# Attention with routed experts on one core: the opening re-ordered and loaded over two queues, and two moves in VectorE's list

## The chip, the cores and the metric

The kernel runs on one core of one Trainium2 chip. TensorE (PE) multiplies matrices, VectorE (DVE), ScalarE (ACT) and GpSimd (POOL) work elementwise, and SyncE (SP) issues most of the transfers; ScalarE and GpSimd issue some as well. The metric is the device time of one execution in microseconds (us). A kernel is run several times and the median counts.

## The reference

```
scores = q @ k.T / sqrt(64)                      # 8 batches x 8 heads, 576 x 576, head size 64
cum    = cumsum(max(s, 0))                       # one gate row s of 576 values per head
scores = where(causal, -1e9, scores + min(-(cum_i - cum_j), 0))
attn   = softmax(scores);  x = attn @ v          # 4608 tokens of 512 values
logits = x @ w_gate;  e = argmax(logits)         # 8 experts, the best one only
out    = p_e * (max(x @ w1[e], 0) @ w2[e])       # 512 -> 1024 -> 512 per token
```

All data are float32. Products keep their accuracy by splitting a number into a rounded high part and a low part: low = number - high, so one product costs three matmuls.

## The kernel before

The 64 heads are taken as 32 pairs, two heads on the two halves of the 128 partitions. A pair goes through five groups of query rows (128 rows each and a mixed group of the last 64 of both heads). For a group g the program does S (scores: the gate term from `cu` and `pick`, then three matmuls from q and k, lines 238 onward), Z (VectorE adds the mask, negates and takes the row maximum, L278), X (ScalarE's exponential, L292), T (transposition on TensorE, L296), C (copy out of PSUM, L321 on VectorE and L322 on ScalarE) and, after all groups, AV (product with v, L332) and XB (copy of the result, L321). Scores live in a PSUM tile `s` of which there are two; a new S, or one of the routing steps RA to RD, may start when the older tile has been read.

Four pairs make a batch of tokens. Its routing runs in eight steps strewn into later rounds: gate products (L375), their transposition (L296, s<-ident,LT), `part`, `both`, `L`, `mx`, `dd` on VectorE (L389 to L406), an exponential on ScalarE (L408), one-hot rows, rank products (L427 to L430), the update of `base` (L436, L439) and `dsi` (L444), and scatters of rows into a table `xs` by GpSimd (L465). `scale` (L351 to L354) takes the reciprocals of the softmax sums; in VectorE's list it is called SC, and SE is the same work done once early, for the seventh of the eight batches.

Four strings in `ORDER`, one per engine, say in which order an engine takes its steps in a round, and how many rounds a step lags behind the first one (`Z1+2` is Z of group 1 of the pair two rounds back). `loop` walks them: an engine's next step is emitted as soon as what it needs has been emitted, so the lists alone set each engine's order.

The opening, `Attention.__init__`, prepares the gate terms: the rows s are loaded twice into `raw` (each half of the partitions holds one head, each copied), VectorE takes max (L138), a running sum (L139), the centres `cen` (L141, L144) and `low` (L147), ScalarE writes five centred copies `cu` (L177, `center`) and VectorE finishes each (L184, `build`). `split` rounds q and k of the first pair on ScalarE (L212, L218) and takes the low parts on VectorE (L215, L222; for later pairs on GpSimd). `raw`, `cum`, `zz` and `low` are parts of the tile `aT[1]`, so the order rows call them aT. Meanwhile TensorE runs products of zeros (L159) so that it is not idle before the first scores, and GpSimd writes masks and constants, among them those of `constants`, whose first part runs before the first round and whose other parts are taken by the step CO.

After the attention the experts run one after the other, TensorE nearly without a pause.

Of the kernel before, what the change touches and what calls it, by code (L numbers as in the profile page):

```python
# [8 lines left out]
F32 = mybir.dt.float32  # L9
# [4 lines left out]
AF = mybir.ActivationFunctionType  # L14
ALU = mybir.AluOpType
# [26 lines left out]
}  # L42
ZB = 4
RUNP = NPAIR
WARM = 24
FIRST = (0, 2, 1, 3, 5, 4)
EVAC = {0: "V", 1: "V", 2: "A", 3: "A", 4: "V"}
STEPS = (3, 0, 1, 4, 5, 6, 2, 7)
# [19 lines left out]
def after(tc, inst, names):  # L68
    ins = getattr(inst, "ins", inst)
    for name in names:  # L70
        tc.add_manual_dep(
            ins, name, mybir.DependencyInfo(mybir.DependencyClass.Sync, mybir.DependencyReason.DATA),
            reason="rows written before",
        )


class Attention:
    def __init__(self, ctx, tc, K, qkv, s, rt, ps_t):
        self.tc, self.nc, self.K, self.qkv, self.rt, self.ps_t = tc, tc.nc, K, qkv, rt, ps_t
# [24 lines left out]
        keep(nc.vector.tensor_reduce(
            out=self.sel, in_=K["ident"].rearrange("p (a c) -> p c a", c=32), op=ALU.add, axis=AX.X
        ))
        s4 = s.rearrange("(p h) c -> h p c", h=2)
        for x in range(4):
            nc.sync.dma_start(raw[32 * x : 32 * x + 32], s4[x // 2])
        self.load(0)  # L110
        for i in range(2):
            nc.scalar.activation(
                self.qd[i].rearrange("p a h c -> p (a h c)"), zz[:, : 4 * HP], AF.Copy
            )
        for x in range(4):
            nc.gpsimd.memset(sign[32 * x : 32 * x + 32, 0:1], 8.0 - 16.0 * (x % 2))
            nc.gpsimd.memset(sign[32 * x : 32 * x + 32, 1:2], 8.0 * (x % 2))
        nc.gpsimd.memset(self.half, 0.0)
        for h in range(2):
            nc.gpsimd.memset(self.half[64 * h : 64 * h + 64, h], 1.0)  # L120
        self.mask = cp.tile([P, 640], F32, name="mask")
        self.mask8 = cp.tile([P, S], F32, name="mask8")
        nc.gpsimd.memset(self.mask, 0.0)
        nc.gpsimd.memset(self.mask8, 0.0)
        nc.gpsimd.affine_select(
            out=self.mask[:, 512:], in_=self.mask[:, 512:], pattern=[[-1, P]],
            compare_op=ALU.is_ge, fill=BIG, base=0, channel_multiplier=1,
        )
        for h in range(2):
            r = slice(64 * h, 64 * h + 64)  # L130
            nc.gpsimd.affine_select(
                out=self.mask8[r, 512:], in_=self.mask8[r, 512:], pattern=[[-1, 64]],
                compare_op=ALU.is_ge, fill=BIG, base=0, channel_multiplier=1,
            )
        self.split(0, 5)
        for part in (0, 2):
            self.split(0, part)
        keep(nc.vector.tensor_scalar(out=raw, in0=raw, scalar1=0.0, scalar2=None, op0=ALU.max))  # L138
        keep(nc.vector.tensor_tensor_scan(out=cum, data0=raw, data1=zz, initial=0.0, op0=ALU.add, op1=ALU.add))  # L139
        mid = cum[:, TC[0] : TC[0] + 4 * TC[1] + 1 : TC[1]]  # L140
        keep(nc.vector.tensor_scalar(  # L141
            out=self.cen[:, 0], in0=mid, scalar1=sign[:, 0:1], scalar2=-1.0, op0=ALU.mult, op1=ALU.mult
        ))
        keep(nc.vector.tensor_scalar(out=self.cen[:, 1], in0=mid, scalar1=sign[:, 1:2], scalar2=None, op0=ALU.mult))  # L144
        for g in ORD:
            self.center(g)
        keep(nc.vector.tensor_scalar(out=low, in0=cum, scalar1=sign[:, 1:2], scalar2=None, op0=ALU.mult))  # L147
        for part in (1, 3):
            keep(self.split(0, part))
        self.build(ORD[0])  # L150
        self.build(ORD[1])
        self.build(ORD[2])
        self.split(0, 4)

        warm = self.ps_s.tile([P, 2, 512], F32, name="s")[:, 0]
        zb = zz.bitcast(BF16)
        for x in range(WARM):
            for c in ((0, 256), (256, 512)) if x % 3 == 0 else ((0, 512),):
                nc.tensor.matmul(  # L159
                    warm[:, c[0] : c[1]], zb[:, :P], zb[:, P + c[0] : P + c[1]],  # L160
                    start=True, stop=True, skip_group_check=True,
                )
        nc.gpsimd.memset(self.Es[MIX][:, S:], 0.0)
        self.LT = rt.tile([P, 640], F32, name="LT", bufs=1)
        nc.gpsimd.memset(self.LT[:, S:], 0.0)
        self.xb, self.sums, self.sumx, self.rr, self.ra = [], [], [], [], []
        for i in range(2):
            self.xb.append(rt.tile([P, 4, 640], F32, name=f"xb{i}", bufs=1))
            nc.gpsimd.memset(self.xb[i][:, :, S:], 0.0)
            self.sums.append(rt.tile([P, 4, 8], F32, name=f"sums{i}", bufs=1))  # L170
            self.sumx.append(rt.tile([P, 4], F32, name=f"sumx{i}", bufs=1))
            self.rr.append(rt.tile([P, 5, 8], F32, name=f"rr{i}", bufs=1))
            nc.gpsimd.memset(self.rr[i][:, 4], 1.0)
            self.ra.append(rt.tile([P, 2, 5, 4], F32, name=f"ra{i}", bufs=1))

    def center(self, g):
        self.nc.scalar.activation(  # L177
            self.cu[:, TO[g] : TO[g] + TW[g]], self.cum[:, : TW[g]], AF.Identity,
            scale=self.sign[:, 0:1], bias=self.cen[:, 0, g : g + 1],
        )  # L180

    def build(self, g):
        o = slice(TO[g], TO[g] + TW[g])
# [22 lines left out]
    def split(self, p, part):  # L206
        nc = self.nc
        d = self.st[p]
        q, k = d["x"][:, :S], d["x"][:, S:]
        if part == 0:  # L210
            d["q"] = self.lq.tile([P, 2, S], F32R, name="q")
            nc.scalar.activation(d["q"][:, 0], q, AF.Copy)  # L212
        elif part == 1:
            e = nc.gpsimd if p else nc.vector
            return e.tensor_tensor(out=d["q"][:, 1], in0=q, in1=d["q"][:, 0].bitcast(F32), op=ALU.subtract)  # L215
        elif part == 2:
            d["kh"] = self.ld.tile([P, S], F32R, name="kh")
# [400 lines left out]
    def loop(self):  # L618
# [3 lines left out]
        self.XR, self.rq, self.sq, self.chain = {}, [], [], None  # L622
        self.R = {b: dict(b=b, xb=self.xb[b % 2]) for b in range(RUNP // 4)}
        self.plan()
        self.todo = constants(self.nc, self.const, self.K, self.wg)
        self.unbuilt = list(ORD[3:])
        done = self.done = {(f"K{x}", 0) for x in range(6)} | {("LX", 0), ("LV", 0), ("LX", 1), ("LV", 1)}
        lists = [[(x.split("+")[0], int(x.split("+")[1])) for x in o.split()] for o in ORDER.values()]
# [359 lines left out]
            if more:  # L988
                self.tails(e, x4)

def constants(nc, cp, K, wg):
    blank = cp.tile([P, WIDE], F32, name="blank")[:, :ROW]
    nc.gpsimd.memset(blank[:, : DM + 1], 0.0)
    nc.gpsimd.iota(blank[:, DM + 1 :].bitcast(I32), pattern=[[0, 1]], base=1 << 20, channel_multiplier=0)
    K["blank"] = blank
    K["wg"] = cp.tile([P, 4, 32], F32, name="wg")
    nc.sync.dma_start(K["wg"], wg.rearrange("(k p) e -> p k e", p=P))

# [113 lines left out]
```

## Time and profile before

| What | us |
|---|---|
| three runs: median (lowest, highest) | 785.6 (785.55, 787.28) |
| the profiled execution, its own time | 784.42 |
| its span from the first to the last instruction | 782.7 |
| TensorE busy | 758.6 |
| VectorE, ScalarE, GpSimd busy | 477.2, 414.7, 219.6 |
| the granted TensorE clock over the span | 0.996 of full |

The profiled execution takes 1.7 us more than its span. A row of the timeline gives the start of an instruction, its duration, engine, line, operation, what it writes and reads, and in brackets how long the engine stood idle before it and what ended that wait. [...] The two ends of the attention matter here: the first 20 us, and the round that begins about 280 us in.

### The profile page before, as it was taken

Reading aid. Unit: us, or ns where it says so; the run is one execution under the profiler, and the core shown is the slowest. Engines: PE = TensorE matmul, PEld = TensorE weight load, DVE = VectorE, ACT = ScalarE, POOL = GpSimd, SP = SyncE. Lnnn points to the kernel's source line nnn. Section 1 sums busy time; section 2 is a strip of 40 time slices with the busy share of each in tenths; the row PEclk is TensorE's granted clock in tenths of the full one; section 3 lists DMA queues with packets and bytes.
Section 4 is the critical chain, followed back from the end, with each engine's and each line's share of the span. In section 5 each row is a group of like instructions: output and inputs, shape, how many; then the busy total and the mean of one; then the engine's idle time right before and its main releaser. Section 6 shows DMA issues by size and latency. Waiting matters only on the chain.

```text
span 782.7 us, 17835 instructions
## 1 busy us (share of the span) xinstructions
PE 758.6 (97%) x6972; PEld 624.4 (80%) x6972; DVE 477.2 (61%) x1247; ACT 414.7 (53%) x1002; POOL 219.6 (28%) x328
## 2 busy tenths in 40 slices
PE   7999999999999988999999999999999999999995
PEld 5888888888888867678788887888888888888874
DVE  7778989899999999655263544522642453633520
ACT  7998888888888866523251432412521431513410
POOL 7544455656564645321001011010011001010011
PEclk9999999999999999999999999999999999999998
DMA  7763234434343414575172642710630271720101
GB/s 263 220 217 99 96 123 131 137 116 150 103 151 107 163 53 149 189 242 201 49 249 95 212 153 87 273 44 16 218 134 28 97 259 57 255 95 22 54 29 41
DMA packets 43903, 105.24 MB, mean 134 GB/s; under 512 B 3983, under 2 KB 3983, under 8 KB 43792
## 3 DMA queue, kind: packets, MB, share of 16 engines
q1 hardware_dynamic: 35408, 80.13, 30.6%
q0 software_dynamic: 5936, 18.92, 6.5%
q10 hardware_dynamic: 2448, 4.74, 1.8%
q8 instruction: 67, 1.10, 0.6%
q14 instruction: 44, 0.36, 0.2%
HBM read 75.91 MB, written 28.12 MB: 133 GB/s over the span
## 4 chain that ended last, share of the span: by engine, by line
issue 37%; DMA 12%; PE 4%; another core or an unknown queue 4%; POOL 3%; DVE 2%; POOLq 1%; ACT 1%; DVEq 0%
DMA xs<-xr,dsi 6%; DMA out_dram<-y,xr 6%; POOL out_dram L853 2%; PE t L332 1%; PE ph L820 1%; PE s L238 1%; PE t L296 0%; DVE z L278 0%; ACT aT L322 0%; POOLq L946 0%; DVE dd L406 0%; POOLq L853 0%; DVE xb L321 0%; POOLq L1107 0%
## 5 line engine op out<-in xcount | busy, mean ns | idle before, releaser
L846 PE MATMUL py<-w2t,hT 128*128 128x512 f32 x768 | 181.3, 392 | 1.2 <-DVEq L960 1.2
L820 PE MATMUL ph<-xT,w1t 128*128 128x512 f32 x768 | 178.3, 391 | 0.6 <-PEq L949 0.6
L820 PEld LDWEIGHTS ph<-xT,w1t 128*128 128x128 f32 x768 | 143.2, 188 | 31.9 <-issue 2.3
L292 ACT ACTIVATE E<-z,m 128x128 f32<-128x128 f32 (+4 forms) x288 | 165.8, 580 | 3.1 <-DVE m L278 3.1
L846 PEld LDWEIGHTS py<-w2t,hT 128*128 128x128 f32 x768 | 142.6, 188 | 30.4 <-issue 1.5
L853 POOL DMA_INDIRECT out_dram<-y,xr x39 | 37.9, 972 | 393.6 <-DVE y L852 331.0
L278 DVE CUSTOM_DVE_ANT_0 z<-s,mask 128x128 f32<-128x128 f32 (+4 forms) x288 | 139.0, 516 | 6.4 <-ACT E L292 0.6
L852 DVE TENSOR_SCALAR y<-py,xr 128x512 f32<-128x512 f32 x35 | 26.3, 751 | 117.5 <-PE py L846 117.5
L332 PE MATMUL t<-aT,v 128*64 128x64 f32 (+2 forms) x1408 | 95.2, 291 | 0.1
L822 ACT ACTIVATE hT<-ph 128x512 fp32r<-128x512 f32 x64 | 38.1, 596 | 96.4 <-PE ph L820 96.0
L332 PEld LDWEIGHTS t<-aT,v 128*64 128x64 f32 x1408 | 66.6, 137 | 18.8 <-issue 2.8
L825 DVE SCALAR_TENSOR_TENSOR hT<-ph,hT 128x512 fp32r<-128x512 f32 x64 | 44.2, 690 | 60.7 <-ACT hT L822 60.6
L238 PE MATMUL s<-kh,q 64*128 64x512 f32 (+3 forms) x512 | 80.2, 318 | 0.0
L322 ACT COPY aT<-t 128x1024 f32<-128x1024 f32 x64 | 57.5, 898 | 38.0 <-PE t L296 38.0
L238 PE MATMUL s<-cu,pick 64*128 64x128 f32 (+4 forms) x320 | 71.9, 374 | 2.5 <-DVE base L439 1.2
L296 PEld LDWEIGHTS t<-ident,E 64*128 64x128 f32 x1600 | 63.8, 138 | 9.2 <-ACT E L292 2.7
L296 PE MATMUL t<-ident,E 64*128 64x64 f32 x1600 | 67.4, 223 | 2.4 <-ACT E L292 0.9
L730 ACT ACTIVATE xT<-t 128x512 fp32r<-128x512 f32 x32 | 18.4, 597 | 90.9 <-PE t L793 90.9
L321 DVE COPY aT<-t 128x256 f32<-128x256 f32 (+2 forms) x96 | 61.6, 641 | 3.9 <-PE t L296 3.5
L292 ACT ACTIVATION_READ_ACCUMULATOR E<-z,m 128x1 f32 x288 | 55.3, 192 | 0.0
L238 PEld LDWEIGHTS s<-cu,pick 64*128 64x128 f32 (+1 forms) x320 | 36.6, 186 | 22.3 <-issue 10.1
L215 POOL TENSOR_TENSOR q<-qk,q 128x576 fp32r<-128x576 f32 x31 | 44.2, 1426 | 32.1 <-ACT q L212 32.0
(159 smaller groups left out, 1016.6 us busy)
## 6 DMA issues: line engine op xcount, KB each, us to landing
raw<-in_w_dram SPq DMA_DIRECT2D x32, 1024.0 KB, 5.8
qk<-in_qkv_dram SPq DMA_DIRECT2D x32, 576.0 KB, 3.9
v<-in_qkv_dram SPq DMA_DIRECT2D x32, 320.0 KB, 4.3
xr<-xs SPq DMA_DIRECT2D x8, 1028.0 KB, 5.7
xs<-blank ACTq DMA_DIRECT2D x9, 514.0 KB, 5.8
xs<-blank SPq DMA_DIRECT2D x8, 514.0 KB, 4.3
xr<-xs SPq DMA_DIRECT2D x8, 514.0 KB, 8.6
xs<-xr,dsi POOLq DMA_INDIRECT x40, 3.4
```

Of the source, the lines that this page charges most:

```text
L215: return e.tensor_tensor(out=d["q"][:, 1], in0=q, in1=d["q"][:, 0].bitcast(F32), op=ALU.subtract)
L238: self.nc.tensor.matmul(out, terms[n][0], terms[n][1], start=n == 0, stop=n == len(terms) - 1, skip_group_check=True)
L278: ins = nc.vector.tensor_tensor_reduce(out=cut(z[:, :w]), in0=x, in1=mask, scale=-0.125, scalar=3.0e38, op0=ALU.add, op1=ALU.min, accum_out=m,
L292: nc.scalar.activation(out, z[:, :w], AF.Exp, bias=m, scale=-1.0, accum_out=total)
L296: self.nc.tensor.transpose(out, src[r], self.K["ident"][r, r])
L321: return self.nc.vector.tensor_copy(o, i)
L322: return self.nc.scalar.copy(o, i)
L332: nc.tensor.matmul(ps[64 * h : 64 * h + 64, bank, lo - 512 * bank : hi - 512 * bank], v[:, kt, h], self.aT[p % 2][:, kt, h, lo:hi], start= ...
L820: nc.tensor.matmul(ps, w[:, a, d, c], x[:, b, d], start=n == 0, stop=n == 11)
L825: nc.vector.scalar_tensor_tensor(out=h[:, 1, f], in0=ps, scalar=0.0, in1=h[:, 0, f].bitcast(F32), op0=ALU.max, op1=ALU.subtract)
L846: self.nc.tensor.matmul(ps, hT[:, a, f, c], w[:, b, f % 4], start=f == 0 and i == 0, stop=f == 7 and i == 2)
L853: disjoint(self.tc, "out", self.nc.gpsimd.indirect_dma_start(out=self.out, out_offset=IndirectOffsetOnAxis(ap=row[:, DM + 1 : DM + 2].bitc ...
```

## The change

In the opening the s rows are loaded by two transfers instead of four, one issued by SyncE and one by ScalarE, each with a source of two copies of 32 rows. q and k of the first pair become two transfers, again one on each queue. ScalarE takes the first centred copy before q and k, and VectorE finishes it before the low parts of q and k. GpSimd writes `half` first, then the first `pick`, and one mask, a strip of `E4` and the first constant wait for the low part of k (`begun`); strips of `LT`, `xb` and `rr` and the other constants move into later CO steps (`blanks`). The products of zeros are 18 blocks of 512 columns instead of 24, 14 of them cut into halves. In VectorE's list SE moves from the end of one round behind the RAd and RDd of the next, and CI moves ahead of Z2 and RCd.

```
-    "DVE": "RAd+4 RDd+4 C4+3 Z1+2 ... RBd+3 Z2+2 RCd+3 CI+3 C1+2 XB+3 Z0+1 CO+1 SE+3",
+    "DVE": "RAd+4 RDd+4 SE+4 C4+3 Z1+2 ... RBd+3 CI+3 Z2+2 RCd+3 C1+2 XB+3 Z0+1 CO+1",
-WARM = 24
+WARM = 18
...
+        nc.gpsimd.memset(self.half, 0.0)
+        for h in range(2):
+            nc.gpsimd.memset(self.half[64 * h : 64 * h + 64, h], 1.0)
         s4 = s.rearrange("(p h) c -> h p c", h=2)
-        for x in range(4):
-            nc.sync.dma_start(raw[32 * x : 32 * x + 32], s4[x // 2])
-        self.load(0)
+        x = self.ldx.tile([P, 2 * S], F32, name="qk")
+        for i, queue in enumerate((nc.sync, nc.scalar)):
+            queue.dma_start(raw[64 * i : 64 * i + 64], s4[i].unsqueeze(0).broadcast_to([2, 32, S]))
+        for i, queue in enumerate((nc.sync, nc.scalar)):
+            queue.dma_start(x[:, S * i : S * i + S], self.qkv[0][:, S * i : S * i + S])
+        self.st[0] = dict(x=x)
+        self.split(0, 5)
...
-        for g in ORD:
+        self.center(ORD[0])
+        for part in (0, 2):
+            keep(self.split(0, part))
+        for g in ORD[1:]:
             self.center(g)
         keep(nc.vector.tensor_scalar(out=low, in0=cum, scalar1=sign[:, 1:2], scalar2=None, op0=ALU.mult))
+        self.build(ORD[0])
         for part in (1, 3):
-            keep(self.split(0, part))
-        self.build(ORD[0])
+            ins = self.split(0, part)
+            keep(ins)
+        self.begun = getattr(ins, "ins", ins).name
+        after(tc, nc.gpsimd.memset(self.mask8, 0.0), [self.begun])
...
-            for c in ((0, 256), (256, 512)) if x % 3 == 0 else ((0, 512),):
+            for c in ((0, 256), (256, 512)) if x < 14 else ((0, 512),):
...
-        nc.gpsimd.memset(self.Es[MIX][:, S:], 0.0)
+        after(tc, nc.gpsimd.memset(self.Es[MIX][:, S:], 0.0), [self.begun])
...
+    def blanks(self):
+        nc = self.nc
+        rest = constants(self.tc, self.const, self.K, self.wg, self.begun)
+        yield next(rest)
+        nc.gpsimd.memset(self.LT[:, S:], 0.0)
+        for i in range(2):
+            nc.gpsimd.memset(self.xb[i][:, :, S:], 0.0)
+            nc.gpsimd.memset(self.rr[i][:, 4], 1.0)
+        yield
+        yield from rest
...
-        self.todo = constants(self.nc, self.const, self.K, self.wg)
+        self.todo = self.blanks()
...
-    nc.gpsimd.memset(blank[:, : DM + 1], 0.0)
+    after(tc, nc.gpsimd.memset(blank[:, : DM + 1], 0.0), [begun])
     nc.gpsimd.iota(blank[:, DM + 1 :].bitcast(I32), pattern=[[0, 1]], base=1 << 20, channel_multiplier=0)
     K["blank"] = blank
+    yield
```

ScalarE's instructions from the program's start, before (qd is a tile of zeros, cu the centred gate terms, kh and q the rounded k and q):

```order
L112 ACT_TABLE_LOAD
L112 ACTIVATE qd_107<-aT_115 128x256
L112 ACTIVATE qd_108<-aT_115 128x256
L212 ACTIVATE q<-qk 128x576
L218 ACTIVATE kh<-qk 128x576
L177 ACTIVATE cu<-aT_115,cen,sign 128x128
L177 ACTIVATE cu<-aT_115,cen,sign 128x256
```

The same engine and place now:

```order
L113 DMA aT_115<-in_s_dram 64x1x576
L115 DMA qk<-in_qkv_dram 128x576
L119 ACT_TABLE_LOAD
L119 ACTIVATE qd_107<-aT_115 128x256
L119 ACTIVATE qd_108<-aT_115 128x256
L191 ACTIVATE cu<-aT_115,cen,sign 128x128
L226 ACTIVATE q<-qk 128x576
L232 ACTIVATE kh<-qk 128x576
L191 ACTIVATE cu<-aT_115,cen,sign 128x256
```

Two transfers stand at the head, and the first cu stands ahead of q and kh.

VectorE in the round that begins about 280 us in, before (rr and ra are the reciprocals of the sums, t and base belong to the ranks):

```order
L278 ISA z,m<-s,mask 128x128
L278 ISA m 128x1
L351 TENSOR_SCALAR rr_221<-sums_219 128x32
L351 TENSOR_SCALAR rr_221<-sumx_220 64x4 x2
L352 RECIPROCAL rr_221<-rr_221 128x32
L353 RECIPROCAL rr_221<-rr_221 64x8
L354 COPY ra_223<-rr_221 128x40
L436 TENSOR_TENSOR t_6275<-s,base 128x40
L439 TENSOR_TENSOR base<-base,s 128x8
L321 COPY aT_114<-t 128x2x5x64
```

The same place now:

```order
L292 ISA z,m<-s,mask 128x128
L292 ISA m 128x1
L450 TENSOR_TENSOR t_6268<-s,base 128x40
L453 TENSOR_TENSOR base<-base,s 128x8
L365 TENSOR_SCALAR rr_218<-sums_216 128x32
L365 TENSOR_SCALAR rr_218<-sumx_217 64x4 x2
L366 RECIPROCAL rr_218<-rr_218 128x32
L367 RECIPROCAL rr_218<-rr_218 64x8
L368 COPY ra_219<-rr_218 128x40
L335 COPY aT_114<-t 128x2x5x64
```

The update of base stands ahead of the gate sums, which were ahead of it.

VectorE later in the same round, before (part, both, L, mx and dd are the routing's logits, z the scores of group 2, xr a batch's scaled rows):

```order
L389 TENSOR_TENSOR part<-s,ra_223 128x160 x2
L278 ISA z,m<-s,mask 128x384
L278 ISA m 128x1
L278 ISA z,m<-s,mask 128x384
L278 ISA m 128x1
L454 TENSOR_TENSOR xr<-s,rr_221 128x2x4x64
L397 TENSOR_TENSOR both<-part 128x160
L399 TENSOR_REDUCE L<-both 128x40
L405 TENSOR_REDUCE mx<-L 128x5
L406 TENSOR_TENSOR dd<-L,mx 128x40
L321 COPY aT_115<-t 128x2x4x64
L321 COPY xb_224<-t 128x576
```

The same place now:

```order
L403 TENSOR_TENSOR part<-s,ra_219 128x160 x2
L411 TENSOR_TENSOR both<-part 128x160
L413 TENSOR_REDUCE L<-both 128x40
L419 TENSOR_REDUCE mx<-L 128x5
L420 TENSOR_TENSOR dd<-L,mx 128x40
L292 ISA z,m<-s,mask 128x384
L292 ISA m 128x1
L292 ISA z,m<-s,mask 128x384
L292 ISA m 128x1
L468 TENSOR_TENSOR xr<-s,rr_218 128x2x4x64
L335 COPY aT_115<-t 128x2x4x64
L335 COPY xb_220<-t 128x576
```

The four instructions from both to dd now follow part at once, ahead of the scores of group 2 and of xr.

## Rows read from the trace of the kernel before

**Rows 1.** Busy time by stretch: us, sum and count of each engine, clock, DMA share, GB/s

```profile
0.00:20.00 20.00, 15.75 (x143) 10.77 (x145) 15.96 (x43) 14.54 (x33) 15.58 (x49) 1.00 0.76 265
20.00:100.00 80.00, 79.53 (x1243) 66.43 (x1238) 66.58 (x223) 72.14 (x200) 37.15 (x65) 1.00 0.47 153
```

**Rows 2.** What TensorE waited for, 180 to 300 us: total, times, longest

```profile
PE s L296 <- DVE m L278: 2.4, 1, 2.4
PE s L238 <- DVE base L439: 1.2, 1, 1.2
```

**Rows 3.** Timeline of all engines, 0 to 16 us

```profile
0.82 1.79 SPq L109 DMA_DIRECT2D aT<-in_s_dram  x4
...
1.60 7.31 PE L159 MATMUL s<-aT 128*128 128x256 bf16 x32 [1.60 <-DVE aT L103]
...
4.32 0.46 DVE L138 TENSOR_SCALAR aT<-aT 128x576 f32<-128x576 f32 x1 [1.75 <-DMA aT<-in_s_dram]
...
4.82 1.36 DVE L139 TENSOR_TENSOR_SCAN aT<-aT 128x576 f32<-128x576 f32 x1
...
6.21 0.60 DVE L141 TENSOR_SCALAR cen<-aT,sign 128x5 f32<-128x5 f32 x1
...
6.50 0.68 ACT L212 ACTIVATE q<-qk 128x576 fp32r<-128x576 f32 x1 [3.67 <-DMA qk<-in_qkv_dram]
...
9.09 0.33 PE L238 MATMUL s<-cu,pick 64*128 64x128 f32 x2 [0.18 <-POOL pick L230]
...
11.76 0.38 ACT L292 ACTIVATE E<-z,m 128x128 f32<-128x128 f32 x1
...
11.93 1.41 POOL L215 TENSOR_TENSOR q<-qk,q 128x576 fp32r<-128x576 f32 x1 [1.16 <-ACT q L212]
...
11.99 1.76 DVE L184 SCALAR_TENSOR_TENSOR cu<-aT,cen,cu 128x384 fp32r<-128x384 f32 x1
...
14.39 0.72 ACT L292 ACTIVATE E<-z,m 128x512 f32<-128x512 f32 x1 [0.79 <-DVE m L278]
```

**Rows 4.** DMA issues, 0 to 20 us: count, KB each, median us to landing

```profile
aT<-in_s_dram SPq DMA_DIRECT2D x4, 72.0 KB, 1.9
```

**Rows 5.** Busy time by stretch as in rows 1, half a microsecond of the opening

```profile
6.00:6.50 0.50, 0.50 (x5) 0.32 (x4) 0.46 (x4) 0.00 (x0) 0.50 (x4) 1.00 1.00 397
```

**Rows 6.** Timeline of all engines, 280.5 to 297 us

```profile
281.07 1.01 DVE L351 TENSOR_SCALAR rr<-sums 128x32 f32<-128x32 f32 x1
...
282.32 1.02 PE L296 MATMUL t<-ident,E 64*128 64x64 f32 x26
...
284.03 0.19 DVE L436 TENSOR_TENSOR t<-s,base 128x40 f32<-128x40 f32 x1
284.25 0.16 DVE L439 TENSOR_TENSOR base<-base,s 128x8 f32<-128x8 f32 x1
...
285.45 0.42 DVE L278 CUSTOM_DVE_ANT_0 z<-s,mask 128x256 f32<-128x256 f32 x1 [0.30 <-PE s L238]
...
289.55 0.55 DVE L389 TENSOR_TENSOR part<-s,ra 128x160 f32<-128x160 f32 x2
...
290.63 2.97 PE L332 MATMUL t<-aT,v 128*64 128x64 f32 x44
...
291.56 0.32 DVE L397 TENSOR_TENSOR both<-part 128x160 f32<-128x160 f32 x1
...
292.25 1.44 POOL L215 TENSOR_TENSOR q<-qk,q 128x576 fp32r<-128x576 f32 x1
...
292.62 2.50 DVE L406 TENSOR_TENSOR dd<-L,mx 128x40 f32<-128x40 f32 x1
...
293.62 1.42 POOL L222 TENSOR_TENSOR kl<-qk,kh 128x576 fp32r<-128x576 f32 x1
...
295.64 0.74 DVE L321 COPY xb<-t 128x576 f32<-128x576 f32 x1
...
296.85 0.34 PE L296 MATMUL s<-ident,xb 64*128 64x64 f32 x4 [2.39 <-DVE m L278]
```

More of the change, by code (lines that the diff above doesn't have):

```diff
@@ L117, in __init__ @@
             nc.gpsimd.memset(sign[32 * x : 32 * x + 32, 1:2], 8.0 * (x % 2))
-        nc.gpsimd.memset(self.half, 0.0)
-        for h in range(2):
-            nc.gpsimd.memset(self.half[64 * h : 64 * h + 64, h], 1.0)
         self.mask = cp.tile([P, 640], F32, name="mask")
@@ L123, in __init__ @@
         nc.gpsimd.memset(self.mask, 0.0)
-        nc.gpsimd.memset(self.mask8, 0.0)
         nc.gpsimd.affine_select(
@@ L128, in __init__ @@
         )
[L129 to L137, printed above, removed]
         keep(nc.vector.tensor_scalar(out=raw, in0=raw, scalar1=0.0, scalar2=None, op0=ALU.max))
@@ L144, in __init__ @@
         keep(nc.vector.tensor_scalar(out=self.cen[:, 1], in0=mid, scalar1=sign[:, 1:2], scalar2=None, op0=ALU.mult))
-        for g in ORD:
+        self.center(ORD[0])
+        for part in (0, 2):
+            keep(self.split(0, part))
+        for g in ORD[1:]:
             self.center(g)
         keep(nc.vector.tensor_scalar(out=low, in0=cum, scalar1=sign[:, 1:2], scalar2=None, op0=ALU.mult))
+        self.build(ORD[0])
         for part in (1, 3):
-            keep(self.split(0, part))
-        self.build(ORD[0])
+            ins = self.split(0, part)
+            keep(ins)
+        self.begun = getattr(ins, "ins", ins).name
+        after(tc, nc.gpsimd.memset(self.mask8, 0.0), [self.begun])
+        for h in range(2):
+            r = slice(64 * h, 64 * h + 64)
+            nc.gpsimd.affine_select(
+                out=self.mask8[r, 512:], in_=self.mask8[r, 512:], pattern=[[-1, 64]],
+                compare_op=ALU.is_ge, fill=BIG, base=0, channel_multiplier=1,
+            )
         self.build(ORD[1])
@@ L162, in __init__ @@
                 )
-        nc.gpsimd.memset(self.Es[MIX][:, S:], 0.0)
+        after(tc, nc.gpsimd.memset(self.Es[MIX][:, S:], 0.0), [self.begun])
         self.LT = rt.tile([P, 640], F32, name="LT", bufs=1)
-        nc.gpsimd.memset(self.LT[:, S:], 0.0)
         self.xb, self.sums, self.sumx, self.rr, self.ra = [], [], [], [], []
@@ L168, in __init__ @@
             self.xb.append(rt.tile([P, 4, 640], F32, name=f"xb{i}", bufs=1))
-            nc.gpsimd.memset(self.xb[i][:, :, S:], 0.0)
             self.sums.append(rt.tile([P, 4, 8], F32, name=f"sums{i}", bufs=1))
@@ L172, in __init__ @@
             self.rr.append(rt.tile([P, 5, 8], F32, name=f"rr{i}", bufs=1))
+            self.ra.append(rt.tile([P, 2, 5, 4], F32, name=f"ra{i}", bufs=1))
+    def blanks(self):
[5 more added lines that the diff above has]
+            nc.gpsimd.memset(self.xb[i][:, :, S:], 0.0)
             nc.gpsimd.memset(self.rr[i][:, 4], 1.0)
-            self.ra.append(rt.tile([P, 2, 5, 4], F32, name=f"ra{i}", bufs=1))
+        yield
+        yield from rest
     def center(self, g):
-        self.nc.scalar.activation(
+        self.tc.keep_in_program_order(self.nc.scalar.activation(
             self.cu[:, TO[g] : TO[g] + TW[g]], self.cum[:, : TW[g]], AF.Identity,
             scale=self.sign[:, 0:1], bias=self.cen[:, 0, g : g + 1],
-        )
+        ))
     def build(self, g):
@@ L211, in split @@
             d["q"] = self.lq.tile([P, 2, S], F32R, name="q")
-            nc.scalar.activation(d["q"][:, 0], q, AF.Copy)
+            return nc.scalar.activation(d["q"][:, 0], q, AF.Copy)
         elif part == 1:
@@ L217, in split @@
             d["kh"] = self.ld.tile([P, S], F32R, name="kh")
-            nc.scalar.activation(d["kh"], k, AF.Copy)
+            return nc.scalar.activation(d["kh"], k, AF.Copy)
         elif part == 3:
@@ L989, in run, with constants @@
                 self.tails(e, x4)
-def constants(nc, cp, K, wg):
+def constants(tc, cp, K, wg, begun):
+    nc = tc.nc
     blank = cp.tile([P, WIDE], F32, name="blank")[:, :ROW]
-    nc.gpsimd.memset(blank[:, : DM + 1], 0.0)
+    after(tc, nc.gpsimd.memset(blank[:, : DM + 1], 0.0), [begun])
     nc.gpsimd.iota(blank[:, DM + 1 :].bitcast(I32), pattern=[[0, 1]], base=1 << 20, channel_multiplier=0)
     K["blank"] = blank
+    yield
     K["wg"] = cp.tile([P, 4, 32], F32, name="wg")
```

2 rows, old and new, of the table ORDER are left out of this document.

## The prediction

> **What bounds the kernel now.** I read the table of busy time by stretch first. From 20 to 100 us TensorE works 79.53 of 80 us, in the first 20 us 15.75 of 20 [rows 1]. Past the ramp TensorE sets the pace, so a microsecond taken from one of its stops, or added to its start, goes through to the end. The list of TensorE's waits shows where the middle has stops: two in one round, 2.4 us behind VectorE's m and 1.2 us behind base [rows 2]. Both moves in VectorE's list lie there. The third view is the timeline of the opening. There ScalarE works without a gap from 6.50 to the first exponentials at 11.76 and stops once, 0.79 us, ahead of 14.39 [rows 3]; a shift of ScalarE's start shifts the ramp, and TensorE with it.
>
> **The round at 280 us: base ahead of the gate sums.** TensorE's scores of group 1 wait 1.2 us for base [rows 2], which VectorE updates from 284.03 to 284.41, behind gate sums that began at 281.07 [rows 6]. Now base comes first and is done about 281.07 + 0.35 = 281.4, ahead of the end of TensorE's transpositions, 282.32 + 1.02 = 283.34 [rows 6]. The whole 1.2 us goes there, but VectorE's gate sums last as long as before, and only the 0.30 us that base took after them (284.03 to 284.33) and the 0.30 us that VectorE then waited for TensorE at 285.45 are gained on its side [rows 6]. The next scores stand behind VectorE's reading of group 1, so I count 0.6 us of 1.2.
>
> **The same round: both to dd behind part.** dd takes 2.50 us at 292.62, while t, of the same 128x40, takes 0.19 at 284.03 [rows 6]. Beside it GpSimd runs q and kl, 292.25 to 295.04, and dd ends with kl. I read that as dd being kept from its operands. Behind dd stand VectorE's copies and the row maxima that free the score tile, for which TensorE waits 2.39 us at 296.85. In the new order dd begins where part ends: 289.55 + 0.55 = 290.10, and both, L and mx need 292.62 - 291.56 = 1.06, dd 0.19, so it ends at 291.35, 0.9 us ahead of GpSimd's q at 292.25 [rows 6]. GpSimd reaches q behind scatters that wait for VectorE's dsi just ahead of part, so the two shift together. What is late next is AV: xb copies its result, ready at 290.63 + 2.97 = 293.60; TensorE went 296.85 - 295.64 = 1.21 after xb began, now 294.81 at the earliest [rows 6]. That gains 2.04 us. Delaying the scores of group 2 by the 1.25 us of the moved four costs nothing, as they still end ahead of 293.60. Both moves: 2.6 us; bounds 0.6 (dd is still held) and 1.2 + 2.4 = 3.6 (both stops vanish whole). I take 2.7, near the sum.
>
> **The opening: when s arrives.** Everything hangs on `raw`. Before, four transfers issue from 0.82 in 1.79 us, each landing 1.9 us after its issue, and VectorE starts at 4.32 [rows 3, 4], which is 0.2 us behind the last landing (0.82 + 3 x 0.45 + 1.9 = 4.1). Each had 32 rows outermost. Now each of the two has a source of 2 copies of 32 rows, against 64 rows in SBUF. No transfer in this trace has so small an outermost count, so its cost is bounded from both sides. With all 16 DMA engines busy the core moves 397 GB/s [rows 5], 24.8 GB/s for one. A 72 KB transfer needs 0.2 us of that, so 1.7 us of the 1.9 is fixed.
> Low end: the 295 KB of both transfers spread over 16 engines, 0.74 us; landing 0.82 + 1.7 + 0.74 = 3.3, VectorE at 3.5.
> High end: a transfer is cut by its outermost count, two engines carry both transfers, 295 KB / 49.6 GB/s = 5.9 us; landing 8.4, VectorE at 8.6.
> By rows alone the low end is nearer, since its kin land in 1.9 us; but all these kin have outermost counts that 16 divides, so they do not speak against a cut in two. I take the high end, because the source gives nothing but the 2 to cut by.
> [...]
>
> **What follows from it.** From VectorE's start to cen written takes 6.21 + 0.60 - 4.32 = 2.5 us before [rows 3]; GpSimd's strips no longer stand beside it, and at 0.2 us for cen it is 2.1. So ScalarE's first centred copy runs at 8.6 + 2.1 = 10.7, and in its fixed order q, k and all that follows stand behind it, where before q began at 6.50. ScalarE has the same work up to the first exponential, 11.76 - 6.50 = 5.26 us [rows 3], so it gets there at 16.0: 4.2 us late. Some comes back. VectorE's last copy of cu took 1.76 us at 11.99 beside GpSimd's q of 11.93, and ScalarE's 0.79 us stop hangs on it [rows 3]; GpSimd now has mask8, a strip and a constant ahead of that q and may come later than VectorE. I take half, 0.4. Loss: 3.8 us; bounds 3.4 and 4.2 without what a cooled TensorE may add.
> q and k, 590 KB behind s, are covered: at 397 GB/s 1.5 us, the two slow engines' share done by about 9.9, ahead of 10.7. The zero products shrink from 12288 to 9216 columns, so from 7.31 us to 5.5 to 6.0 [rows 3], ending near 7.4; the first scores come 4.2 us later than before, near 13.3 with their low part of k. TensorE's pause there is hidden behind ScalarE, unless its clock drops.
> The constants moved to later rounds cost nothing: VectorE reads PSUM there, and GpSimd works 37.15 of 80 us [rows 1].
>
> **Sum.** 784.42 + 3.8 - 2.7 = 785.5 for an execution like the profiled one. The median of the runs lies 1.2 above that execution (785.6), so 786.7.
>
> **Rivals.**
> 1. Sixteen engines carry s. VectorE starts at 3.5, ScalarE at 5.6 instead of 6.50, 0.9 us gained, up to 0.8 more if VectorE's cu escapes q; I take 1.2. 785.6 - 1.2 - 2.7 = 781.7, range 780.8 to 782.8. For it: every transfer seen behaves so, and the opening was arranged around an early s. Against it: the cut of two.
> 2. The cut is real, but the two queues use different engines: 147 KB / 49.6 = 3.0 us, VectorE at 5.7, ScalarE at 7.8, 1.3 late, 0.4 back. 785.6 + 0.9 - 2.7 = 783.8. Against it: nothing in the trace tells queues apart by engines.
> [...]
> 4. dd is held by GpSimd all the same, with group 2's maxima now behind it: only 0.6 of the 2.7 stays. 785.6 + 3.8 - 0.6 = 788.8. Against it: 0.9 us of room.
>
> **How the numbers follow.** About 0.3%, 2.4 us, is what a measurement of this kernel can tell from no change. Chances: forecast 0.57 (786.7, its own range 785.2 to 788.0), rival 1 0.25, rival 2 0.06, rival 3 0.08, rival 4 0.04. Faster than 783.2: rival 1 whole and a little of rival 2, 0.26. Slower than 788.0: rivals 3 and 4 and a tenth of the forecast's, less what of rival 3 stays small, 0.16. Within: 0.58. The range runs from inside rival 1, 781.0, to inside rival 3, 788.8, and leaves out about 0.05 below and 0.1 above.
>
> **What would show it.** The two transfers of s landing about 7.5 us after issue, VectorE's max near 8.6 and the first exponential near 16.0 show the opening right; a max at 3.5 makes it wrong and the kernel faster. dd at about 0.2 us and a stop of under 0.6 us in place of the 2.39 show the round right; a dd of 2 us shows it wrong. [...]

## The result and the profile after

The changed kernel takes 790.38 us (median of five, 789.33 to 790.91) where the kernel before takes 785.60 in the same runs: ratio 1.0055 [1.0038, 1.0071], 4.8 us slower. The profiled execution took 790.91 us (span 789.2) against 784.42 before. 786.7 was predicted, with 788.8 as the upper end.

The busy time by stretch, columns as in [rows 1], shows where it went: TensorE works 7.21 of the first 20 us, where it worked 15.75.

```profile
0.00:20.00 20.00, 7.21 (x42) 5.14 (x44) 6.10 (x12) 5.36 (x9) 4.36 (x24) 0.78 0.62 172
20.00:100.00 80.00, 78.94 (x1180) 66.66 (x1181) 66.11 (x221) 72.31 (x200) 42.32 (x83) 0.97 0.51 164
12.00:15.00 3.00, 0.00 (x0) 0.00 (x0) 0.55 (x2) 0.00 (x0) 0.00 (x0) 0.50 0.14 52
17.00:25.00 8.00, 6.72 (x36) 5.46 (x36) 7.08 (x21) 8.00 (x20) 6.05 (x12) 0.50 0.38 123
```

The timeline of the opening (start, duration, engine, operation; in brackets the idle time ahead and what ended it) answers to [rows 3]:

```profile
0.81 0.74 SPq L113 DMA_DIRECT2D aT<-in_s_dram  x1
0.81 1.45 ACTq L113 DMA_DIRECT2D aT<-in_s_dram  x1
1.60 5.49 PE L165 MATMUL s<-aT 128*128 128x256 bf16 x32 [1.60 <-DVE aT L103]
...
14.41 0.46 DVE L132 TENSOR_SCALAR aT<-aT 128x576 f32<-128x576 f32 x1 [12.52 <-DMA aT<-in_s_dram]
...
16.38 0.23 DVE L135 TENSOR_SCALAR cen<-aT,sign 128x5 f32<-128x5 f32 x1
...
16.64 0.49 ACT L191 ACTIVATE cu<-aT,cen,sign 128x128 fp32r<-128x128 f32 x1 [11.93 <-DVE cen L135]
...
17.78 0.47 PE L252 MATMUL s<-cu,pick 64*128 64x128 f32 x2 [10.70 <-DVE cu L198]
...
21.89 0.39 ACT L306 ACTIVATE E<-z,m 128x128 f32<-128x128 f32 x1
...
33.80 2.54 PE L346 MATMUL t<-aT,v 128*64 128x64 f32 x40
```

VectorE's first work on s begins at 14.41 instead of 4.32, the first exponential at 21.89 instead of 11.76, TensorE's first AV (t<-aT,v, its end of the ramp) at 33.80. In the kernel before that last row reads:

```profile
23.63 2.97 PE L332 MATMUL t<-aT,v 128*64 128x64 f32 x44
```

TensorE is 10.17 us late at the end of the ramp, and still 10.24 late at the AV ahead of the round (286.82 against 276.58). At the next two AVs, inside the round, this falls to 8.64 and then 6.71. Here are these three AVs now, and the first and the third of them in the kernel before (the second is the 290.63 of [rows 6]):

```profile
286.82 2.97 PE L346 MATMUL t<-aT,v 128*64 128x64 f32 x44
...
299.28 2.97 PE L346 MATMUL t<-aT,v 128*64 128x64 f32 x44
...
310.90 2.97 PE L346 MATMUL t<-aT,v 128*64 128x64 f32 x44
```
```profile
276.58 2.97 PE L332 MATMUL t<-aT,v 128*64 128x64 f32 x44
...
304.18 2.97 PE L332 MATMUL t<-aT,v 128*64 128x64 f32 x44
```

There it stays: 6.70 at the last AV, 6.5 us in the spans. So the opening lost 10.2 us and the round gave back 3.54 (10.24 - 6.70).

The list of TensorE's waits from 186 to 309 us, the stretch of [rows 2], has neither the 2.4 us behind m nor the 1.2 us behind base:

```profile
PE s L310 <- DVE part L403: 0.8, 1, 0.8
PE s L389 <- DVE m L292: 0.5, 1, 0.5
PE s L310 <- DVE m L292: 0.4, 1, 0.4
```

The 0.5 us ahead of L389, the gate products, is shorter too. In the kernel before that stop was 0.80:

```profile
281.21 1.18 PE L375 MATMUL s<-xb,wg 128*32 128x288 f32 x16 [0.80 <-DVE m L278]
```

And the timeline of the round, the rows that answer to [rows 6]:

```profile
291.19 0.16 DVE L453 TENSOR_TENSOR base<-base,s 128x8 f32<-128x8 f32 x1
...
298.19 0.55 DVE L403 TENSOR_TENSOR part<-s,ra 128x160 f32<-128x160 f32 x2
...
299.82 0.20 DVE L420 TENSOR_TENSOR dd<-L,mx 128x40 f32<-128x40 f32 x1
...
300.90 1.44 POOL L229 TENSOR_TENSOR q<-qk,q 128x576 fp32r<-128x576 f32 x1
...
303.56 0.47 PE L310 MATMUL s<-ident,xb 64*128 64x64 f32 x8 [0.45 <-DVE m L292]
```

dd takes 0.20 us instead of 2.50 and is over 0.88 us ahead of GpSimd's q; TensorE's stop behind m is 0.45 us instead of 2.39.

**Two engines, seen in the packets.** The DMA view from 0 to 20 us (busy share of the 16 engines in tenths and GB/s, by half microseconds; then issues):

```profile
DMA  0000037979999999989999962111115898973110
GB/s 0 0 0 0 9 46 166 314 241 357 328 250 290 244 240 263 220 239 246 247 331 323 277 200 63 48 48 55 55 41 97 223 321 319 409 177 78 51 45 20
...
aT<-in_s_dram SPq DMA_DIRECT2D x1, 144.0 KB
aT<-in_s_dram ACTq DMA_DIRECT2D x1, 144.0 KB
```

From 12 to 15 us a share of 0.14 is busy (0.14 x 16 = 2.2) and the core moves 52 GB/s: two engines of sixteen. The trace's single packets agree. In the kernel before, sixteen packets of 4 bytes follow each transfer of s (the first sixteen from 2.05 to 2.35 us); I read them as the ends of its engines' shares. On ScalarE's queue there are now eighteen for s and k. Fourteen come from 5.68 to 6.78, for k alone; two at 13.51 and 13.94, for s; two more at 15.60 and 16.04, for the rest of k. That the count of 2 would put s on two engines was an estimate of the prediction, which no row of the kernel before shows; here the packets show it.

What the prediction did not see is the rate of these two. A row of s (2304 bytes) takes 0.093 us where the engines run alone (the median from 13 to 14 us), which is the 24.8 GB/s of its sum. But from 6 to 10 us rows of 2304 bytes from SyncE's queue and from ScalarE's go through the two engines in turn (seven of each from 7 to 8 us), and each takes 0.14 to 0.17 us (medians by microsecond); on the other fourteen, rows of 4608 bytes take 0.29 to 0.33 us, against 0.18 in the kernel before from 4 to 8 us. The core moves 220 to 290 GB/s there with every engine busy, not 397. From 12 us the two are alone with what is queued: a row of s, 0.093, then a row of v or qk, 0.102 or 0.18, and so on.

### The profile page after: what moved, and what is told of

Read it like the earlier page. It is cut to its first block, busy times and chain, and to the rows that moved or that the text cites. A ratio compares the mean times of both kernels' runs of the same rounds, so it can differ in the third digit from the quotient of the medians.

```text
span 789.2 us, 17833 instructions
## 1 busy us (share of the span) xinstructions
PE 759.6 (96%) x6972; PEld 626.7 (79%) x6972; DVE 473.3 (60%) x1247; ACT 415.2 (53%) x1002; POOL 218.5 (28%) x328
## 4 chain that ended last, share of the span: by engine, by line
PE 37%; issue 37%; DMA 14%; another core or an unknown queue 4%; POOL 3%; DVE 2%; ACT 1%; POOLq 1%; ACTq 0%; DVEq 0%
PE s L252 16%; PE t L346 12%; DMA xs<-xr,dsi 6%; DMA out_dram<-y,xr 6%; PE t L310 6%; POOL out_dram L867 2%; DMA qk<-in_qkv_dram 2%; PE s L310 2%; PE ph L834 1%; PE s L389 1%; DVE z L292 1%; ACT aT L336 1%; ACT E L306 1%; DVE rr L365 0%
## 5 line engine op out<-in xcount | busy, mean ns | idle before, releaser
L252 PE MATMUL s<-cu,pick 64*128 64x128 f32 (+4 forms) x320 | 72.9, 380 | 10.8 <-DVE cu L198 10.7
```

Source lines behind the costliest of these rows:

```text
L252: self.nc.tensor.matmul(out, terms[n][0], terms[n][1], start=n == 0, stop=n == len(terms) - 1, skip_group_check=True)
```

## The experiments

Unless the text says otherwise each kernel is the changed one with the edit shown. The kernel before ran beside each of them and took 791 to 793 us (medians) instead of 785.6. So what counts is a kernel's ratio to the kernel before beside it, and the starts in the traces. The first two columns and AV are starts in us; AV is TensorE's first AV, 23.58 in a profile of the kernel before from these runs (before_again).

| run | VectorE's max on s | first exponential | AV | ratio to before |
|---|---|---|---|---|
| after_again | 14.25 | 21.72 | 34.04 | 1.0076 [1.0062, 1.0091] |
| s_16_rows | 3.92 | 11.64 | 22.63 | 0.9934 [0.9920, 0.9949] |
| s_alone | 10.07 | 18.96 | 31.08 | 1.0035 [1.0020, 1.0050] |
| both_on_sync | 13.34 | 20.82 | 32.11 | 1.0081 [1.0062, 1.0101] |
| both_on_sync_held | 10.62 | 18.09 | 30.02 | 1.0034 [1.0021, 1.0047] |
| s_16_behind_qkv | 9.50 | 16.97 | 28.96 | 1.0021 [1.0009, 1.0032] |
| s_two_halves | 13.86 | 21.34 | 32.6 | not compared |
| warm_to_17 | 14.35 | 21.83 | 34.57 | 1.0063 [1.0042, 1.0083] |

**The changed kernel again (after_again).** 

> The changed kernel again, beside before and the other runs of this call. By its first result 4.8 us over before. On the chip of the earlier calls the list's two moves gave more (4.7 in place of 3.5 us), and the opening costs 10.2 us in TensorE's start: 10.2 - 4.7 = 5.5 us over before, first exponential near 21.9. Rival: the loss of the opening is partly hidden there and it is level with before.

797.31 us against 790.96, 6.4 us slower; against before_again TensorE is 10.4 us late ahead of the round and 5.9 at the end. The theory holds, at 5.9 to 6.4 for 5.5.

**Is the cut of s the loss? (s_16_rows).**

```diff
-            queue.dma_start(raw[64 * i : 64 * i + 64], s4[i].unsqueeze(0).broadcast_to([2, 32, S]))
+            for j in (2 * i, 2 * i + 1):
+                queue.dma_start(raw[32 * j : 32 * j + 32], s4[i])
```

> The changed kernel with s loaded by four transfers of 32 rows, two on each queue, in place of two transfers whose source is 2 copies of 32 rows. My theory (only the two-engine cut of s is late in the opening): VectorE's max at 3.5 to 4, first exponential near 11.2, 0.5 us ahead of the kernel before; 785.6 - 3.5 - 0.5 = 781.6. Rival (the rest of the opening costs something too: two DMA issues ahead of ScalarE's table load, q and k halves of rows of 2304 bytes, pauses of TensorE): first exponential at 12.5 or later and 783 or more.

787.69 us against 792.77: 5.1 us faster than before, where the changed kernel was 6.4 slower.

```profile
3.92 0.46 DVE L133 TENSOR_SCALAR aT<-aT 128x576 f32<-128x576 f32 x1 [2.03 <-DMA aT<-in_s_dram]
...
11.64 0.39 ACT L307 ACTIVATE E<-z,m 128x128 f32<-128x128 f32 x1
...
22.63 2.97 PE L347 MATMUL t<-aT,v 128*64 128x64 f32 x44
```

The same bytes in four transfers of 32 rows (sixteen engines by the packets of the kernel before; the core moves 332 GB/s from 2.5 to 3.0 us) are there at 3.92, and TensorE reaches its first AV 0.95 us ahead of before. This 0.95 is no more than one opening differs from run to run: list_alone below, with the opening of the kernel before, has its first AV at 24.62. But nothing of the 10 us is left, so the whole loss is the cut of s. (The first exponential came at 11.64, not 11.2: cen is 2.2 us behind the max as in the changed kernel, and q then begins at 6.78, 0.14 us behind the end of the first cu.)

**What the two engines take alone (s_alone).** v, and q and k of pairs 0 to 4, are held until s has been read:

```diff
+        ins = nc.vector.tensor_scalar(out=raw, in0=raw, scalar1=0.0, scalar2=None, op0=ALU.max)
+        keep(ins)
+        self.seen = getattr(ins, "ins", ins).name
 ...
+            after(tc, queue.dma_start(self.st[0]["x"][:, S * i : S * i + S], ...), [self.seen])
```

> The changed kernel with every load of q, k and v of the first five pairs held until VectorE has read s, so that the two engines carry s and nothing else. Theory A (the landing at 14.2 instead of 8.4 is the share of the later loads on the same two engines): s lands at about 8.4, the max is near 8.6, q and k come about 3 us behind that and the first exponential near 16.5; about 786 to 787. Rival B (two engines move these rows at less than 24.8 GB/s each, whatever is queued behind): the max stays at 13 or later, and q and k come later still; 793 or more.

The DMA view of this run, GB/s by half microseconds from 0 to 20, and VectorE's max in its timeline:

```profile
GB/s 0 0 0 0 9 33 79 58 51 46 51 51 51 51 51 48 49 49 43 4 0 0 0 92 166 387 415 391 414 450 406 360 412 468 384 442 369 433 398 382
```
```profile
10.07 0.46 DVE L130 TENSOR_SCALAR aT<-aT 128x576 f32<-128x576 f32 x1 [8.17 <-DMA aT<-in_s_dram]
```

Two engines move 46 to 51 GB/s from 4 to 9 us, about the 49.6 of the prediction. (The small load of the gate weights, issued at 1.61, runs beside s here, in rows of 128 bytes at 0.013 us each.) Each engine moves one row of s at 2.31, and the others follow only from 3.50, not from the 2.5 that the prediction counts from (0.82 + 1.7); the last ends at 9.53. So s by itself is read 1.5 us later than predicted, and the other 4.3 us of the 14.41 come with the other loads. The pause from 2.31 to 3.50 is this run's own: in the changed kernel the rows of s go on from 2.30. Why it is there stays open. Theory A holds in kind. q and k, issued only at 10.5, made the exponential late, 18.96 instead of 16.5, so the total says nothing.

**The turns of two queues, or the work of the other engines? (both_on_sync, both_on_sync_held).** Both transfers of s on SyncE's queue; in the second, in addition, v and later pairs held as in s_alone, q and k of the first pair not.

```diff
-        for i, queue in enumerate((nc.sync, nc.scalar)):
-            queue.dma_start(raw[64 * i : 64 * i + 64], ...)
+        for i in range(2):
+            nc.sync.dma_start(raw[64 * i : 64 * i + 64], ...)
```

> The changed kernel with both transfers of s (2 copies of 32 rows each) on SyncE's queue; k alone stays on ScalarE's. Theory A (an engine takes its queues in turn, and a queue's rows in order: s is late in the changed kernel because each of its 32 rows per engine on ScalarE's queue lets a row of what SyncE has queued pass): 64 rows of 0.093 us on each of two engines, begun at 2.3, and 8 rows of k let in, 0.75: VectorE's max at 9.0 to 9.6, first exponential near 16.7, so 5 us late in place of 10; some 5 us faster than the changed kernel, within 1.5 us of before. Rival B (the two engines share their time among all that is queued, by bytes): max at 13 or later, as slow as the changed kernel.

> Both transfers of s on SyncE's queue as in the run both_on_sync, and the loads of v and of q and k of pairs 1 to 4 held until VectorE has read s; q and k of the first pair are not held. The order within SyncE's queue up to q is that of both_on_sync. In that run the rows of s were first in their queue, yet VectorE's max came at 13.34, since 64 rows per engine took about 0.16 us each. Theory A (each row of s is slowed by what the other fourteen engines move at that time): with nothing else to move after q and k, rows at 0.093 us, max at 9.3 to 10.2, first exponential near 17.2. Rival B (two transfers of one queue share the two engines with the rows queued behind them, or the rows are slow in themselves): max still at 12 or later.

The busy time from 6 to 9 us (the last two columns are DMA share and GB/s) and the max. both_on_sync:

```profile
6.00:9.00 3.00, 1.54 (x11) 0.75 (x8) 0.00 (x0) 0.00 (x0) 0.00 (x0) 1.00 1.02 273
```
```profile
13.34 0.46 DVE L132 TENSOR_SCALAR aT<-aT 128x576 f32<-128x576 f32 x1 [11.44 <-DMA aT<-in_s_dram]
```

both_on_sync_held:

```profile
6.00:9.00 3.00, 2.58 (x13) 1.36 (x10) 0.00 (x0) 0.00 (x0) 0.00 (x0) 1.00 0.13 50
```
```profile
10.62 0.46 DVE L132 TENSOR_SCALAR aT<-aT 128x576 f32<-128x576 f32 x1 [8.72 <-DMA aT<-in_s_dram]
```

My theory for the first failed: with s at the head of one queue its max came at 13.34, not 9.0 to 9.6. But the rows of s were first in their order: from 7 to 11 us 14 rows of 2304 bytes pass in a microsecond at 0.15 us each, which is the whole time of two engines. The second run says why. With the other fourteen engines idle from 5.5 us on the same rows take 0.095, 21 a microsecond, and the max is at 10.62. So 2.7 us of the lateness come from work on the other engines, beside which each row takes half as long again. The remaining 1.1 (13.34 to 14.41; 0.9 against the 14.25 of after_again) goes with the second queue; that it is the turns the two queues take is argued, not shown by a run of its own. In total both_on_sync came out as slow as the changed kernel, although its AV is 1.9 us earlier than that of after_again: its lateness against before_again fell by 3.2 us after 276 us, that of after_again by 4.5. Its round lost more: from 305 to 315 us the granted clock is 0.71 (0.87 in after_again), and a stop of TensorE behind m at 309.76 takes 2.13 us (1.36 at 310.58). Why that differs stays open.

**What makes the rows slow? (s_16_behind_qkv, s_two_halves).**

```diff
+        self.load_v(0)
+        self.load(1)
+        self.load_v(1)
+        for i, queue in enumerate((nc.sync, nc.scalar)):
+            for j in (2 * i, 2 * i + 1):
+                keep(queue.dma_start(raw[32 * j : 32 * j + 32], s4[i]))
```

> s in four transfers of 32 rows as in the run s_16_rows, but issued behind q and k of the first pair, v of two pairs and q and k of the second. It asks whether rows of s slow the other engines wherever they run. Theory A (two engines working alone at the head of a queue, not the rows of s, go with the lower rate of 250 to 290 GB/s): while s moves, the core moves over 350 GB/s and rows of 2304 bytes take about 0.1 us. Rival B (reading s beside q, k and v is slow): under 300 GB/s in that stretch, rows of s at 0.14 us or more. In both, s lands behind 1.8 MB, near 7.2, VectorE's max near 7.5, first exponential near 15, some 3.5 us slower than s_16_rows.

```profile
GB/s 0 0 0 32 97 249 396 405 413 415 358 373 277 372 405 395 267 249 406 375 408 394 373 214 10 0 0 0 0 0 83 129 304 378 249 37 0 0 0 0
```

Unclear. From 4 to 9 us, while s moves, the core mostly makes 358 to 415 GB/s, as theory A has it. But it makes 277 from 6.0 to 6.5, and from 8 to 9 us, when rows of s run beside rows of 4608 bytes, 267 and 249; these rows then take 0.126 and 0.305 us. So rows that slow each other are not confined to a transfer cut in two. The forecast common to both theories was a miss: the max came at 9.50, not near 7.5, and by the ratios the kernel is some 7 us slower than s_16_rows, not 3.5.

```diff
-            queue.dma_start(raw[64 * i : 64 * i + 64], s4[i].unsqueeze(0).broadcast_to([2, 32, S]))
+            queue.dma_start(raw[64 * i : 64 * i + 64], s4)
```

> The changed kernel with each transfer's source of 2 copies of the same 32 rows replaced by the two different halves of s, so again 2 times 32 rows of 2304 bytes, outermost count 2; half of the partitions hold the other half of s, so the sums and all that follows from them are other numbers. Theory A (the outermost count cuts the transfer, and the slowdown beside other loads has nothing to do with two engines reading the same rows): two engines carry s, landing and max near 14.4 as in the changed kernel. Rival B (the same rows read twice at a time make the rate fall): two engines, but rows at 0.1 us and a max at 10 to 12. Rival C (only a source of copies is confined to as many engines as copies): sixteen engines, max below 4.

Max at 13.86, again two engines (on ScalarE's queue fourteen packets of 4 bytes by 6.41, then two at 12.82 and 13.39), rows of s at 0.12 to 0.16 us from 5 to 11. Theory A: here it was the outermost count of 2, copies or not, and not the reading of the same rows by two engines. (The one run took 810.25 us; with other numbers in it, that time is not compared.) What makes rows slow each other stays open.

**Does the clock cost anything? (warm_to_17).**

```diff
-WARM = 18
+WARM = 67
```

> The changed kernel with 67 zero products in place of 18, so that TensorE works up to about 17.5 us and its clock need not fall ahead of the first scores at 17.8. Theory A (ScalarE's fixed order sets the ramp, and the clock costs next to nothing): score matmuls at full speed, first exponential still near 21.9, 789.8 to 790.4. [...]

The busy time of two stretches (third column from the end: the granted clock):

```profile
17.00:25.00 8.00, 6.45 (x40) 4.33 (x37) 6.93 (x21) 8.00 (x21) 6.11 (x12) 0.79 0.39 121
25.00:34.00 9.00, 8.50 (x98) 7.39 (x98) 5.99 (x21) 7.08 (x20) 6.18 (x15) 0.81 0.70 196
```

The first exponential comes at 21.83, so the granted clock of 0.50 that the changed kernel shows from 17 to 25 us (above) is not what makes it late; theory A. But more zero products didn't save the clock here: it was 0.79 in that stretch and 0.81 in 25 to 34 us, where the changed kernel has 1.00, and AV comes at 34.57, no earlier than 33.80. From the first exponential to AV it is 10.99 us in s_16_rows, with the clock at 1.00 up to 25 us, and 11.91 in the changed kernel. By my estimate, from this difference, 0.9 is about what the fallen clock can have cost; no run isolated it. One pair of profiles comes near. list_alone and before_again have the same opening; in the first the granted clock is 0.57 from 15 to 19 us, in the second 1.00, and from the first exponential to AV they take 12.54 (12.08 to 24.62) and 11.87 us. In total warm_to_17 is as slow as the changed kernel, within the intervals.

**The list alone (list_alone, base_first, dd_first) and the kernel before (before_again).** On the kernel before:

```diff
-    "DVE": "RAd+4 RDd+4 C4+3 ... RBd+3 Z2+2 RCd+3 CI+3 ... CO+1 SE+3",
+    "DVE": "RAd+4 RDd+4 SE+4 C4+3 ... RBd+3 CI+3 Z2+2 RCd+3 ... CO+1",
```

base_first has SE's move alone, dd_first CI's.

> The kernel before with VectorE's new list alone (SE third, CI ahead of Z2); the opening is that of before. My theory (the round gives more than the 2.7 us of the prediction): TensorE's offset against before fell by 3.5 us between AV27 and AV29 of the changed kernel, so 785.6 - 3.5 = 782.1, and both stops (1.2 behind base, 2.4 behind m) are gone here too. Rival: part of that fall came from the late ramp, which put the round elsewhere against its loads; then 2.0 to 2.7 and 783 to 783.6.

> The kernel before, for its profile beside the other runs of this call: where its time differs from the profiled execution shown of before (784.42 us). In the earlier call before ran at 792.77 us and the kernel with the new list alone at 788.06, with an unexplained stop of TensorE of some 3 us near 309. Theory: that stop is there in before as well and has nothing to do with the change, TensorE's waits of 1.2 us behind base and 2.4 us behind m stand in it. Rival: the stop comes with the new list, and before runs from 304 to 313 as in its first profile.

> The kernel before with one of the two moves in VectorE's list alone: base ahead of the gate sums (SE third). By the prediction 0.6 us of the 1.2 us stop comes through to the end; my theory now, from a round that gave 3.55 in place of 2.7: 1.2 whole. Rival: nothing, since VectorE's work is only reordered and its stop behind m takes it back: 0.

> The kernel before with the other of the two moves alone: both, L, mx and dd right behind part, ahead of two row maxima and xr (CI ahead of Z2). By the prediction 2.04 us; my theory now: 2.4, the whole stop behind m. dd at 0.2 us in place of 2.50. Rival: dd is held by GpSimd all the same, 2 us, and nothing is gained.

Times and ratios: list_alone 788.06 us against 792.77, 4.7 less, 0.9939 [0.9924, 0.9954]. base_first 790.89 against 791.78, 0.9 less, 0.9986 [0.9972, 1.0000], so by its time alone hardly told from nothing. dd_first 788.57 against 791.78, 3.2 less, 0.9964 [0.9951, 0.9976]. The list's gain is there without the late ramp. TensorE's waits near the round, in before_again (792.31 us):

```profile
PE s L296 <- DVE m L278: 2.4, 1, 2.4
PE s L238 <- DVE base L439: 1.6, 1, 1.6
```

In base_first:

```profile
PE s L296 <- DVE m L278: 2.4, 1, 2.4
...
PE s L375 <- DVE m L278: 0.8, 1, 0.8
```

In dd_first:

```profile
PE s L238 <- DVE base L439: 1.4, 1, 1.4
...
PE s L296 <- DVE m L278: 0.5, 1, 0.5
```

Each move takes away its own stop and leaves the other. Against before_again TensorE gains 1.24 us in base_first between two AVs (+0.27 to -0.97) and 2.96 in dd_first (+0.03 to -2.93): base is worth 1.24 of a stop of 1.59, dd 1.9 us of its stop and a microsecond more. The clock has a part in that one: behind the stops TensorE's 128x288 scores run slower in before_again (granted clock 0.88 from 295 to 305 us, 1.00 in the first profile of the kernel before):

```profile
302.85 0.45 PE L238 MATMUL s<-kl,qd 128*128 128x288 f32 x1
```

and in dd_first:

```profile
299.15 0.29 PE L238 MATMUL s<-kl,qd 128*128 128x288 f32 x1
```

In base_first the stop ahead of the gate products (L375) is 0.80 us, as in the kernel before, in before_again, list_alone and dd_first. In every kernel with the rest of the change it is 0.45 or 0.46, in s_16_rows too, whose ramp is not late. So these 0.35 us come from an edit outside the list; which one stays open.

list_alone has an unexplained stop of TensorE near 310. before_again has it as well, here at 313:

```profile
313.60 0.53 PE L296 MATMUL t<-ident,E 64*128 64x64 f32 x10 [1.10 <-issue]
```

It is in the kernel before too, so it does not come with the change. The kernel before took longer in these runs, and most of that is lost in this stretch: before_again is 0.2 us behind the first profile at the AV of 276.58, and 6.4 us at the AV of 313.11 (319.54).

## Why the prediction was wrong

- **What bounds it.** Right: a late ramp goes through to the end; 10.17 us at the first AV are 10.24 at the round.
- **The opening, the high end.** This is the step that failed. Two engines for 295 KB was right, as an estimate without a row behind it, and the low end was dropped for it. But "two engines carry both transfers, 295 KB / 49.6 GB/s = 5.9 us; landing 8.4, VectorE at 8.6" was called a high end, and it is a low one: it lets the two engines carry s and nothing else, at the rate of an undisturbed row (0.093 us). Measured in its place: 10.07 with s alone (1.5 later, as its rows begin 1.0 later in that run and the last is read 0.5 after it ends), 13.34 beside other loads on the other engines (2.7 above the 10.62 of the same transfers without them), 14.41 with s on two queues. The prediction knew of what is queued behind: it costed q and k behind s, and not s behind them.
- **From VectorE's start on.** Right to the tenth: cen 2.2 us later for 2.1, then 5.25 us of ScalarE's work to the first exponential for 5.26. The 0.4 that should come back did not: first exponential to AV takes 11.91 us against 11.87 before. VectorE's last cu did get short (0.61 for 1.76), and in s_16_rows 0.9 came back. In the changed kernel the granted clock of 0.50 falls into this stretch; that it took the 0.9 away again is likely, not shown.
- **The loss** so is 10.2 instead of 3.8, far outside its bounds of 3.4 and 4.2, which only held what followed from 8.6 and not the landing itself. That made the range too short on that side.
- **q and k, zero products.** q and k were there in time, though k's last packet came at 16.04 and not by 9.9; the zero products ended at 7.09 for 7.4.
- **base ahead of the gate sums.** Mis-sized: 1.24 us for 0.6. The scores behind VectorE's reading of group 1 did not hold it; the whole stop of 1.22 went. Between the AVs around it the changed kernel gains 1.59, but 0.35 of that is the shorter stop ahead of the gate products, which base_first doesn't have and the prediction didn't count.
- **both to dd.** Right: the stop at 296.85 went from 2.39 to 0.45, 1.94 us for 2.04, dd at 0.20, over 0.88 us ahead of q for 0.9. Together 3.54 for 2.7, just inside the bound of 3.6.
- **Rivals.** Sixteen engines (781.7, 3.9 under before) did not happen but is what s_16_rows is: 5.1 under. Rival 3 of the chances, with the 788.8 that the range runs to, is a slower TensorE clock. No run shows a price for it by itself; the runs showed a granted clock of 0.50 from 17 to 25 us, and by the estimate above it can have cost about 0.9 us of the lateness, so it was not the cause. TensorE stood 10.7 us ahead of its first scores (17.78, not near 13.3). dd was not held.

With the two measured terms the sum closes: 784.42 + 10.2 - 3.54 = 791.1, measured 790.91. That says only that nothing else was lost or gained; both terms are read from the same two traces.

**The version to keep** is s_16_rows, 0.9934 of before. By itself the list gives 0.9939; what the opening adds without the cut, 0.95 us at the first AV, is under what these runs can tell apart.

## What to carry to other kernels

Here a source that begins with a count of 2 put a transfer on two DMA engines, whether the two were copies or not, and how long it then took was set by what else those engines and the others were given (VectorE's max at 10.07, 13.34 or 14.41). So ask what is queued beside a transfer before you call a time by bytes a high end. The same rows in four issues of 32, each some 0.45 us of a queue, brought the data ten microseconds earlier (the max at 3.92 for 14.25). And when one table entry moves work ahead of a stop, look for what else ends within that stop: where nothing did, it went whole.

## What the runs showed of the hardware that was not expected

- The two engines' rows were slower while the other fourteen worked, though from 7 to 11 us rows of s alone filled the time of the two: 0.15 us each in both_on_sync, 0.095 in both_on_sync_held. In the changed kernel the others' rows of 4608 bytes took 0.29 to 0.33 from 6 to 10 us instead of the 0.18 of the kernel before. What is shared was not found.
- An engine with rows on two queues took them one by one in turn: in the changed kernel from 12.6 to 13.2 us rows of s follow each other on an engine at 0.19 to 0.20 us, with one row of v between them (0.093 and 0.102), from 14.1 to 14.9 rows of k at 0.27, with one row of qk (0.093 and 0.18).
- An issue of the cut transfer occupied its queue longer: 1.45 us on ScalarE's and 0.74 on SyncE's, where the four issues of before took 1.79 together.
- Behind a stop of 2.40 us at 297.40 and another of 0.82 at 301.75 TensorE was slower in before_again (0.45 us for 0.29 of a 128x288 score, 0.24 apart for 0.13; granted clock 0.88 from 295 to 305). Behind the one of 2.39 us in the first profile it was not (0.29 us at 300.36; granted clock 1.00).
- With longer zero products (warm_to_17) the granted clock was 1.00 from 17 to 20 us, at the first scores, where the changed kernel had 0.50, and the fall came later, in the ramp itself: 0.79 and 0.81 in the two stretches shown.
